# ISAB attention followed by a maxout-2 layer on one core: a searched list of work is replaced, and copies of m1 move to GpSimd

## The chip, the cores and the metric

The kernel runs on one core of a Trainium2 chip. Its time is the device time of one execution in microseconds (us); before the change the median of three runs is 314.69 us (314.38 to 314.78). One execution was recorded by the hardware profiler; all rows shown are from that trace. PE is TensorE (PEld its loading of weights), DVE is VectorE, ACT is ScalarE, POOL is GpSimd, SP the engine that issues most DMAs.

## What is computed

x has 4 batches of 12544 tokens of 128 channels; inducing has 32 rows. Two attention blocks follow each other (the 32 rows attend to x, then x attends to the 32 results), and each token then goes through a maxout of two linear maps into 1024 and a linear map back to 128.

```python
def mab(q, kv):
    s = scale * (q @ kv.transpose(0, 2, 1))
    a = np.exp(s - s.max(-1, keepdims=True))
    a /= a.sum(-1, keepdims=True) + 1e-09
    return a @ kv
h = mab(I, x)                 # [4, 32, 128]
y = mab(x, h)                 # [4, 12544, 128]
g = np.maximum(y @ w1, y @ w2)  # 1024 wide
out = g @ w_out
```

The kernel uses max(a, b) = a + relu(b - a): with w21 = w2 - w1, out = relu(y w21) w_out + y (w1 w_out). As y is a weighted mean of h, hwd = h w21 and m1 = h w1 w_out are made once for each batch (both have 32 rows, kept four times over, one copy for each quarter of the partitions), and a token needs only its 32 weights e2 (unnormalised), e2 times hwd, relu, and w_out. The division by the sum of the weights comes last, in the eviction.

## The kernel before

**Units of work.** A batch has 98 chunks of 128 tokens. Blocks take up to 16 chunks, four for each of four quarters (32 partitions each); there are 28 blocks. `stage` (word s) computes a block's 32 weights for four quarters (matmuls at L712, exponential on ScalarE). `phase` (word p) takes one piece of work from each of up to four quarters: 512 columns of e2 times hwd in a quarter of the array's rows (matmuls at L1205, all four quarters side by side), each into its own bank of PSUM, then a relu to SBUF by `relu_out`, on ScalarE (L1110) or VectorE (L1107). A piece of a phase can also be replaced by the linear part of an open group (e2 times m1, `linear_of`). `final_one` (a plain number n in the list: n of them) multiplies 128 tokens' relu by one of eight 128x128 blocks of w_out (L989); 8 of them for each chunk add up in a group's bank. There are 108 groups, each the chunks of one block and one quarter. `evict_group` multiplies a finished group by the reciprocals `rp` and writes it into one of 6 buffers of osbs, on VectorE (L1024) or, where EVICT has a 1 for that group, chunk by chunk on ScalarE (L1031); SP then stores it. The last block's groups take their linear part from m1bd by `linear_full` (L963): m1 laid out with a quarter's rows at a time and zeros elsewhere.

**First attention.** For the batches 1 to 3 it is woven into the work of the batch before. x is loaded by DMAs from GpSimd's queue (`load_x`), transposed by DMAs from SP's queue (word x), scored (c: L399, exponential on ScalarE), the exponentials are transposed by DMA (t), and multiplied with x (a: L458). Words r, e, h, w and m (`pool_rest`, `small_rep`, `small_h`, `small_hwd`, `small_m1`) finish a batch's h, hwd and m1. Word g (`turn_e2`) transposes a block's e2 by a DMA from SP's queue, and GpSimd then adds up the 32 weights of each token (L776, four halvings and den) and takes the reciprocal (L780, rd). Where that has not been done when it is needed, `dens` does it on TensorE.

**What sets the order.** All engines' instructions are in program order. The body's order is ORDER, a list of words written out by a search. The class Clock keeps a rough account of time on each engine while the program is built; it has no instructions of its own, but banks of PSUM (`bank`: the one that comes free first), the quarter that issues next and the filling with dummy matmuls (`keep_busy`) are chosen by it. PAIR is its price of a final matmul, SWITCH those of going from one layout of the array to another: full (128 rows: finals and most small matmuls), row (32 rows: phases), col (32 columns: s, c, a).

**The words in detail.** pN.V.H is a phase of N pieces; bit k of V gives the k-th piece's relu to VectorE, otherwise to ScalarE. Bit k of H holds the k-th piece: it takes two neighbouring banks, and if the next phase of the same run brings the following piece of the same quarter into the second bank, one relu takes both (128x1024, `relu_out` with two units). Any word other than p releases the held pieces as single relus (`flush`). `pick` chooses, among the quarters' next pieces, those that the finals need first. The head of the program (transposes, scores and sums of batch 0) is not in the list; the list begins about 22.7 us into the span. There H computes the second half of hwd of batch 0, V transposes w1, W multiplies it with w_out (L662).

Of the kernel before, what the change touches and what calls it, by code (L numbers as in the profile page):

```python
# [12 lines left out]
ALU = mybir.AluOpType  # L13
# [7 lines left out]
class Clock:  # L21


    PAIR = 0.0563
    COLS = 0.0566
    SWITCH = {
        "full": {"row": 0.095, "col": 0.095},
        "row": {"full": 0.082, "col": 0.088},
        "col": {"full": 0.1, "row": 0.094},
    }  # L30
    STEP = 0.0035
# [126 lines left out]
def kernel(  # L158
# [34 lines left out]
    ck = Clock()  # L193
# [73 lines left out]
    m1bd = consts.tile([128, 4, C], F16, name="m1bd")  # L267
# [3 lines left out]
    with tc.manual_schedule(engines={ET.PE, ET.DVE, ET.Activation, ET.Pool, ET.SP}):  # L271
# [25 lines left out]
        st = [dict() for _ in range(B)]  # L297
# [298 lines left out]
        def small_m1(b):  # L596
            bi, ps = bank([128, 512])
            ck.wait(max(ck.bank[bi], st[b]["hT4r"]), "p1")
            nc.tensor.matmul(out=ps[:, 0:128], lhsT=st[b]["hT4"], rhs=w1out, start=True, stop=True)
            end = ck.run(0.06)  # L600
            m1 = smp.tile([128, C], F16, name=f"m1_{b}", tag="m1")
            bd = {B - 1: [0, 1, 2, 3]}.get(b, [])
            outs = [(m1bd[32 * q : 32 * (q + 1), q, :], slice(32 * q, 32 * (q + 1))) for q in bd]
            for o, r in outs + [(m1, slice(0, 128))]:
                if b == 0:
                    nc.vector.tensor_scalar(
                        out=o, in0=ps[r, 0:128], scalar1=st[0]["rw"][r, :], scalar2=None, op0=ALU.mult
                    )
                else:
                    nc.vector.tensor_copy(out=o, in_=ps[r, 0:128])  # L610
                ck.bank[bi] = ck.on_dve(end, 0.28)
            st[b]["m1"] = m1
            st[b]["m1r"] = ck.bank[bi]

        w_of = {}
# [6 lines left out]
        def difference(eng, lo, hi, ready, us):  # L622
            eng.tensor_sub(w21[:, lo:hi], w2f[:, lo:hi], w1f[:, lo:hi])
            w_of["w21", lo] = ck.on_dve(ready, us) if eng is nc.vector else ck.on_pool(ready, us)

        def cast_w1(h):
            sl = slice(512 * h, 512 * (h + 1))
            if h == 0:
                nc.vector.tensor_copy(out=w1h[:, sl], in_=w1f[:, sl])
                ck.on_dve(20.4, 0.33)  # L630
            else:
                nc.gpsimd.tensor_copy(out=w1h[:, sl], in_=w1f[:, sl])
                w_of["cast"] = ck.on_pool(0.0, 0.8)

        def weights_2():
            turned = []
# [201 lines left out]
        bi, ps = bank([128, 512])  # L838
# [46 lines left out]
        difference(nc.gpsimd, 256, 512, 21.0, 0.64)  # L885
        load_x(1, 1)
        load_x(1, 2)
        difference(nc.gpsimd, 512, J, 22.9, 1.25)
        cast_w1(1)
        for i in range(3, 7):  # L890
            load_x(1, i)
# [82 lines left out]
        def final_one(narrow=False):  # L974
# [152 lines left out]
        def phase(n, vector=0, hold=0):  # L1127
# [195 lines left out]
```

## Time and profile before

| | |
|---|---|
| median of 3 runs | 314.69 us (314.38 to 314.78) |
| the profiled execution | 314.68 us, span 312.9 us |
| granted TensorE clock, mean | 0.998 |
| DMA | 55.69 MB, mean 178 GB/s |
| HBM | read 27.28 MB, written 25.69 MB |

The span is from the first to the last instruction; the 1.8 us between it and the execution's time lie before and after it. "Busy" is the union of the instructions' times on an engine. A group's row in the profile gives, after the shapes and the count, the busy time in us and the mean of one in ns, then the engine's idle time just before these instructions and what ended most of it. Matmuls overlap (one of 128 columns is recorded as 219 ns, and the next starts 56 ns later), so TensorE's steps are read here from starts, not from durations. A timeline row gives start, duration, engine, line, operation, output and inputs, shapes and the number of instructions merged; an idle time in front of it stands in brackets. A row of windows gives busy times of PE, PEld, DVE, ACT and POOL with counts, then the granted clock, the DMA share and GB/s. A row of DMA issues ends in the median us from issue to landing.

### The profile page before, as it was taken

Reading aid. Unit: us, or ns where it says so; the run is one execution under the profiler, and the core shown is the slowest. Engines: PE = TensorE matmul, PEld = TensorE weight load, DVE = VectorE, ACT = ScalarE, POOL = GpSimd, SP = SyncE. Lnnn points to the kernel's source line nnn. Section 1 sums busy time; section 2 is a strip of 40 time slices with the busy share of each in tenths; the row PEclk is TensorE's granted clock in tenths of the full one; section 3 lists DMA queues with packets and bytes.
Section 4 is the critical chain, followed back from the end, with each engine's and each line's share of the span. In section 5 each row is a group of like instructions: output and inputs, shape, how many; then the busy total and the mean of one; then the engine's idle time right before and its main releaser. Section 6 shows DMA issues by size and latency. Waiting matters only on the chain.

```text
span 312.9 us, 12567 instructions
## 1 busy us (share of the span) xinstructions
PE 306.0 (98%) x5316; PEld 239.4 (77%) x5316; DVE 273.1 (87%) x485; ACT 280.7 (90%) x581; POOL 122.6 (39%) x183
## 2 busy tenths in 40 slices
PE   6999999999999999999999999999999999999996
PEld 2875777777877777778877887778778877788885
DVE  2458999999889999988999998999999899989894
ACT  3668999999989989999999999989999899998875
POOL 7374007910530006677500565139205743288000
PEclk9999999999999999999999999999999999999999
DMA  7999999999399999989699999993422522342223
GB/s 206 208 255 203 218 214 192 167 231 232 107 204 244 256 212 202 212 199 218 136 241 256 185 241 200 194 229 114 131 86 103 153 102 87 118 130 103 103 88 136
DMA packets 80793, 55.69 MB, mean 178 GB/s; under 512 B 62272, under 2 KB 65632, under 8 KB 80736
## 3 DMA queue, kind: packets, MB, share of 16 engines
q1 hardware_dynamic: 74768, 41.19, 56.5%
q0 software_dynamic: 5968, 13.70, 22.6%
q8 instruction: 41, 0.67, 0.9%
q14 instruction: 16, 0.13, 0.1%
HBM read 27.28 MB, written 25.69 MB: 169 GB/s over the span
## 4 chain that ended last, share of the span: by engine, by line
PE 94%; DMA 3%; DVE 1%; issue 1%; POOL 0%; ACT 0%; POOLq 0%
PE psall L989 61%; PE psall L1205 23%; DMA xn<-in_x_dram 3%; PE psall L712 2%; PE psall L458 1%; PE psall L399 1%; PE psall L309 1%; PE psall L371 1%; PE psall L325 1%; DVE relus L1107 1%; PE psall L571 1%; PE psall L504 0%; PE psall L362 0%; DVE hwd L575 0%; PE psall L819 0%
## 5 line engine op out<-in xcount | busy, mean ns | idle before, releaser
L1110 ACT ACTIVATE relus<-psall 128x512 f16<-128x512 f32 x468 | 239.2, 620 | 15.4 <-PE psall L1205 14.4
L1107 DVE TENSOR_SCALAR relus<-psall 128x512 f16<-128x512 f32 x308 | 195.5, 683 | 16.6 <-PE psall L1205 15.7
L989 PE MATMUL psall<-woutp,relus 128*128 128x128 f16 x3104 | 203.7, 220 | 0.0
L989 PEld LDWEIGHTS <-relus 128*128 128x128 f16 x3104 | 174.9, 98 | 33.1 <-issue 27.3
L1205 PE MATMUL psall<-e,hwd 32*128 32x512 f16 (+2 forms) x840 | 81.1, 362 | 0.0
L776 POOL TENSOR_TENSOR half<-ed 128x256 f32<-128x256 f16 (+2 forms) x22 | 13.4, 611 | 145.5 <-DMA ed<-e 145.5
L780 POOL TENSOR_TENSOR rd<-den,minus 128x16 f32<-128x16 f32 (+2 forms) x22 | 57.8, 2628 | 1.7
L1024 DVE TENSOR_TENSOR osbs<-psall,rd 128x512 f32<-128x512 f32 (+1 forms) x80 | 50.9, 637 | 4.3 <-PE psall L1205 1.3
L1205 PEld LDWEIGHTS <-hwd 32*128 32x128 f16 x880 | 27.9, 91 | 11.7 <-issue 2.3
L1205 PE MATMUL psall<-m,e 32*128 32x128 f16 x372 | 36.6, 216 | 0.0
L1205 PEld LDWEIGHTS <-e 32*128 32x128 f16 x372 | 22.2, 92 | 9.6 <-issue 2.0
L776 POOL TENSOR_TENSOR half<-half 128x32 f32<-128x32 f32 (+4 forms) x66 | 21.4, 324 | 5.2
L228 POOL DMA_DIRECT2D xn<-in_x_dram x32 | 17.8, 569 | 5.7 <-DMA xn<-in_x_dram 4.3
L1024 DVE TENSOR_TENSOR osbs<-psall,rp 128x512 f32<-128x512 f32 (+3 forms) x24 | 15.6, 649 | 0.5 <-PE psall L1205 0.4
L313 DVE COPY xT<-psall 128x512 f16<-128x512 f16 (+3 forms) x12 | 5.7, 485 | 8.6 <-PE psall L309 8.4
L413 ACT ACTIVATE eu<-psall 128x512 f16<-128x512 f32 x18 | 10.8, 612 | 0.3 <-PE psall L399 0.2
L725 ACT ACTIVATE e<-psall 128x512 f16<-128x512 f32 (+2 forms) x21 | 10.9, 574 | 0.1
L316 ACT COPY xT<-psall 128x768 f16<-128x768 f16 (+3 forms) x10 | 5.8, 576 | 4.6 <-PE psall L309 4.5
L309 PE MATMUL psall<-identity,xn 128*128 128x128 f16 x98 | 7.5, 219 | 1.5 <-DMA xn<-in_x_dram 1.0
L712 PE MATMUL psall<-xT,hT 128*32 128x512 f16 (+3 forms) x110 | 8.4, 362 | 0.0
L309 PEld LDWEIGHTS <-xn 128*128 128x128 f16 x98 | 5.5, 97 | 3.1 <-DMA xn<-in_x_dram 1.4
L399 PE MATMUL psall<-xT,inducingT 128*32 128x512 f16 x72 | 6.4, 381 | 0.0
(114 smaller groups left out, 129.8 us busy)
## 6 DMA issues: line engine op xcount, KB each, us to landing
out_dram<-osbs SPq DMA_DIRECT2D x90, 256.0 KB, 2.9
xn<-in_x_dram POOLq DMA_DIRECT2D x24, 448.0 KB, 9.9
out_dram<-osbs SPq DMA_DIRECT2D x10, 128.0 KB, 4.3
relus<-in_moe_w_dram POOLq DMA_DIRECT2D x4, 256.0 KB, 5.7
xn<-in_x_dram POOLq DMA_DIRECT2D x4, 224.0 KB, 10.3
xT<-xn SPq DMA_TRANSPOSE x33, 4.3
relus<-in_x_dram SPq DMA_DIRECT2D x1, 512.0 KB, 4.0
relus<-in_x_dram SPq DMA_DIRECT2D x1, 384.0 KB, 4.4
```

What stands on the lines that cost most here:

```text
L228: nc.gpsimd.dma_start(out=xn_at[b, i][:, 0:n, :], in_=xr[b, :, k0 : k0 + n, :])
L309: nc.tensor.transpose(ps[:, j, :], xn[:, g + j, :], identity16)
L413: nc.scalar.activation(out=eu, in_=ps, func=AF.Exp, scale=scale, accum_out=st[b]["es"][:, u : u + 1])
L712: nc.tensor.matmul(out=ps[32 * q : 32 * (q + 1), 128 * t : 128 * (t + n)], lhsT=hq, rhs=xT[:, c : c + n, :], start=True, stop=True, tile_p ...
L725: nc.scalar.activation(out=blk.e2[:, 0 : 128 * wd], in_=ps[:, 0 : 128 * wd], func=AF.Exp, scale=st[0]["rs"] if blk.b == 0 else scale,)
L776: nc.gpsimd.tensor_tensor(out=dst, in0=cur[:, :, 0:n], in1=cur[:, :, n : 2 * n], op=ALU.add)
L780: nc.gpsimd.tensor_tensor(out=rp[:, 0:wd, :].rearrange("p t q -> p (t q)"), in0=den[:, 0 : 4 * wd], in1=minus1[:, 0 : 4 * wd], op=ALU.pow,)
L989: nc.tensor.matmul(out=g.ps[lo:hi, 128 * c : 128 * (c + 1)], lhsT=relu[:, lo:hi], rhs=woutp[:, jb, :], start=not g.started, stop=(state["m ...
L1024: nc.vector.tensor_mul(osb[:, 0:m, :], g.ps[:, 0 : m * C].rearrange("p (s c) -> p s c", s=m), g.blk.rp[:, t0 : t0 + m, q : q + 1].broadcas ...
L1107: nc.vector.tensor_scalar(out=dst, in0=src, scalar1=0.0, scalar2=None, op0=ALU.max)
L1110: nc.scalar.activation(out=dst, in_=src, func=AF.Relu)
L1205: nc.tensor.matmul(**seq.pop(0))
```

## The change

- Clock's prices: PAIR from 0.0563 to 0.0559, row to full from 0.082 to 0.0985, the cast of w1 on GpSimd from 0.8 to 0.62, one difference from 1.25 to 1.28, with GpSimd's clock set to 22.98 before it.
- `small_m1`: VectorE copies m1 from PSUM at once, and for the last batch the four quarters of m1bd are copied from m1 by GpSimd, instead of from PSUM by VectorE ahead of m1.
- ORDER is another list (words in the same notation). It has the same words s, c, t, a, r, e, h, w, m, H, V, W, x and g, in other places, other phases, other runs of finals, and 69 hold bits, where the list before has none.
- EVICT gives the groups 102 and 105 to ScalarE, instead of 102, 104, 105 and 107.

```diff
--- before.py
+++ after.py
@@ -21,11 +21,11 @@
 class Clock:
 
 
-    PAIR = 0.0563
+    PAIR = 0.0559
     COLS = 0.0566
     SWITCH = {
         "full": {"row": 0.095, "col": 0.095},
-        "row": {"full": 0.082, "col": 0.088},
+        "row": {"full": 0.0985, "col": 0.088},
         "col": {"full": 0.1, "row": 0.094},
     }
     STEP = 0.0035
@@ -600,15 +600,17 @@
             end = ck.run(0.06)
             m1 = smp.tile([128, C], F16, name=f"m1_{b}", tag="m1")
             bd = {B - 1: [0, 1, 2, 3]}.get(b, [])
-            outs = [(m1bd[32 * q : 32 * (q + 1), q, :], slice(32 * q, 32 * (q + 1))) for q in bd]
-            for o, r in outs + [(m1, slice(0, 128))]:
-                if b == 0:
-                    nc.vector.tensor_scalar(
-                        out=o, in0=ps[r, 0:128], scalar1=st[0]["rw"][r, :], scalar2=None, op0=ALU.mult
-                    )
-                else:
-                    nc.vector.tensor_copy(out=o, in_=ps[r, 0:128])
-                ck.bank[bi] = ck.on_dve(end, 0.28)
+            if b == 0:
+                nc.vector.tensor_scalar(
+                    out=m1, in0=ps[:, 0:128], scalar1=st[0]["rw"], scalar2=None, op0=ALU.mult
+                )
+            else:
+                nc.vector.tensor_copy(out=m1, in_=ps[:, 0:128])
+            ck.bank[bi] = ck.on_dve(end, 0.28)
+            for q in bd:
+                r = slice(32 * q, 32 * (q + 1))
+                nc.gpsimd.tensor_copy(out=m1bd[r, q, :], in_=m1[r, :])
+                ck.on_pool(ck.bank[bi], 0.3)
             st[b]["m1"] = m1
             st[b]["m1r"] = ck.bank[bi]
 
@@ -630,7 +632,7 @@
                 ck.on_dve(20.4, 0.33)
             else:
                 nc.gpsimd.tensor_copy(out=w1h[:, sl], in_=w1f[:, sl])
-                w_of["cast"] = ck.on_pool(0.0, 0.8)
+                w_of["cast"] = ck.on_pool(0.0, 0.62)
 
         def weights_2():
             turned = []
@@ -885,7 +887,8 @@
         difference(nc.gpsimd, 256, 512, 21.0, 0.64)
         load_x(1, 1)
         load_x(1, 2)
-        difference(nc.gpsimd, 512, J, 22.9, 1.25)
+        ck.pool = 22.98
+        difference(nc.gpsimd, 512, J, 22.9, 1.28)
         cast_w1(1)
         for i in range(3, 7):
             load_x(1, i)
@@ -1227,33 +1230,34 @@
 
         state["stage"] = 1
         ORDER = """
-        s p4.9 s p2.2 H1 V W p2.2 p4.2 14 m0 p3.1 4 p3.2 4 p3.3 15 p4.2 6 x1.0 2 p3.6 15 p4.8 13 p4.5 14
-        p3.1 x1.1 10 p1 p4.6 14 p4.1 20 p4.5 p2.2 16 s x1.2 s p3.5 15 p4.1 g3 18 g4 p3.4 p2.1 x1.3 11
-        x1.4 p4.5 14 p4.1 14 p3.3 10 p4.5 s c1.0 18 p2.1 g5 p3.1 x1.5 x1.6 6 x1.7 6 p4.9 11 x1.8 12 p3.6
-        p3.4 17 s c1.1 p3.4 12 x1.9 3 p4.12 3 x1.10 4 p3.2 11 p4.1 21 p4.2 p2.1 21 p4.6 t1.1 12 p1 p4.5
-        14 c1.2 c1.3 p4.10 23 p3.2 t1.3 p3.2 23 p4.3 18 p2.1 p4.8 28 p4.12 p2 23 g6 p4.5 a1.1 c1.4 a1.3
-        c1.5 p3.4 11 r1 t1.5 14 p4.8 p3.2 31 p2.1 p4.4 9 a1.5 p4.8 5 e1 17 h1 5 p4.3 p3.1 21 w1 6 s s
-        p4.10 25 p3.1 p3.4 33 p4.3 p3.1 24 s s p3.4 18 p2.2 p4.2 11 m1 13 p3.4 4 p4.12 21 p1 p3.2 15 p2.2
-        p4.2 18 p4.5 15 p1.1 p4.2 x2.0 x2.1 14 x2.2 3 p4.5 6 x2.3 13 x2.4 p4.4 p2.1 14 g9 9 x2.5 p3.6 p2
-        13 p4.9 21 p2.2 p4.2 31 x2.6 x2.7 p3.5 p4.1 26 x2.8 g10 c2.0 s p4.12 21 p2.1 p4.8 23 p4.3 10 p3.3
-        c2.1 s c2.2 13 p3.1 7 t2.1 1 p4.3 8 x2.9 2 g11 x2.10 g12 4 p4.3 16 p4.8 13 p4.12 15 p3.2 15 c2.3
-        p3.4 p3.1 28 p3.4 p3.4 22 p4.5 13 s t2.3 c2.4 a2.1 c2.5 p3.1 p3.1 21 g13 7 p2.1 t2.5 p4.2 28 p2.1
-        p4.10 6 r2 22 p3.6 p3 24 p4.1 a2.3 a2.5 p3.2 5 p4.6 14 p4.1 e2 24 p4.3 p3 12 h2 19 p4.1 p2.1 18
-        p4.10 10 p3.4 12 w2 6 p4.14 s s s 23 p2.2 p4.1 24 p3.6 s p3.2 14 p4.8 8 m2 6 p4.4 23 p3.1 p2.2 12
-        g17 2 x3.0 g15 p4.8 21 p2.1 x3.1 x3.2 p4.8 29 p3.1 x3.3 p4.10 24 p3.4 11 p4.9 x3.4 13 p4.4 16
-        p4.10 21 p3.1 p3.2 11 x3.5 x3.6 g1 g16 10 p4.1 x3.7 21 p2.1 p4.1 31 p3.2 p4.3 29 p4.5 10 x3.8
-        p3.5 s s c3.0 c3.1 13 p4.12 18 p3.3 p2 2 t3.1 9 x3.9 x3.10 3 p4.1 18 p3.5 p3 27 p4.9 p2.1 19 s
-        c3.2 c3.3 a3.1 p4.10 p2.1 19 g19 t3.3 g18 p4.9 21 p3.1 p3.1 20 p4.5 r3 21 p3.2 p3.2 31 p4.14 p3
-        27 p4.12 a3.3 c3.4 c3.5 11 p3.3 p3 8 t3.5 23 g20 p4.8 p3.3 31 p2.1 p4.8 23 p4.6 a3.5 p1 p3.4 10
-        p4.1 2 g7 1 e3 10 g14 7 h3 6 p4.3 p3.2 14 w3 3 m3 5 s s s 11 g21 p1 p4.4 21 p4.10 12 p1 p4.6 15
-        p4.8 19 p2.3 p4.2 28 g23 p2.2 p4.2 19 p3.4 3 g22 19 p3.2 p4.6 39 p3.1 p3.2 31 p4.10 p3.2 31 p4.3
-        p2 22 p4.5 11 p3.1 8 p4.1 17 p4.10 14 p3.6 s s s 11 p4.2 8 p3.5 14 g24 p4.1 16 p4.9 12 p4.1 p1.1
-        g8 23 p4.14 p2 15 s p4.1 21 p4.8 p2.1 30 g27 p4.2 p3.5 20 g26 p4.1 18 g25 3 p2.2 p4.1 31 p3.3
-        p4.4 28 p4.12 p1 17 p4.3 18 p2.2 p4.8 31 p3.4 p4.6 1 g2 30 p2.2 p4.8 31 p3.1 p4.5 32 p4.5 p2 30
-        p4.10 p2 24 p4.8 p2.1 32 p3.6 p3.1 23 p2.3 p4.1 36 p2.1 p3.1 24 p4.1 p4.7 56
+        s p3.6.4 p3.5.3 s H1 V W p2.2 p4.2 10 m0 5 x1.0 p1 p3.3 8 p3 x1.1 p2.3 17 p4.12 7 p3.2 15 p4.8 13
+        p4.12 14 p3.4 9 x1.2 p4.6 p1 14 p4.2 x1.3 21 p4.2 p2.3 18 p3.3 s x1.4 s 15 p4.2 17 p4.5 11 x1.5
+        g3 p3.3 p2.0.1 13 g4 p4.8 14 p3.5 10 p4.6 x1.6 x1.7 s c1.0 18 p2.0.1 p3.5 13 p4.10 21 p3.4 x1.8
+        p3.6.1 17 s c1.1 p3.2 x1.9 14 p4.3 10 p3.1.2 9 g5 p4.4 21 p4.1 p2.1 21 p4.5 11 p1 t1.1 p4.5 14
+        c1.2 c1.3 x1.10 p4.3 21 t1.3 p4.4 p2.1 28 p2.3.3 p4.8 25 p4.3 18 p2.1 p4.2.4 25 p4.11 c1.4 c1.5
+        a1.1 a1.3 p3 9 g6 t1.5 17 p4 p3.7 15 r1 19 p4.5.9 p2.0.3 11 a1.5 p4.1 3 e1 19 h1 3 p3.5 p4.2 10
+        w1 15 s s p4.5 24 p3.0.2 p3.2 31 p4.4.4 p3.6 12 m1 14 s s p3.1 16 p2.2 p4.2 22 p4.9 11 p3.2 13
+        p1.0.1 p3.1 15 p2.2 p4.2 19 x2.0 2 x2.1 p4.5 2 x2.2 13 p2.1.1 x2.3 p3.4 18 p4.5 10 g9 8 p4.2 p2.1
+        23 p2.1 p3.2.1 11 x2.4 p4.6 21 p2.0.2 x2.5 p4.6 32 p4.7 x2.6 p3 28 p4.5 s c2.0 1 x2.7 17 p4.3 g10
+        p2 6 x2.8 16 p4.10 10 p3.5 x2.9 c2.1 c2.2 s 16 t2.1 1 g11 p3.1 6 p4.6 14 p4.6 x2.10 15 p4.2 13
+        p4.9 g12 14 p3.1 15 s c2.3 p3.6 p3.4.4 29 p2.1 p4.4 24 p4.6 10 c2.4 t2.3 a2.1 c2.5 g13 p3.1 p3.1
+        19 t2.5 9 p4.10 p2 28 p2.2 p4.3 r2 28 p3.2 p3.2 23 p4.4 a2.3 a2.5 6 p3.1 p4.12 21 p4.2 14 e2 10
+        p3.5.1 p4.8 21 h2 9 p4.12 p2 21 p4.9 6 w2 4 p3.2 12 p4.12 s s s 22 p2.2.1 p4.2 24 p3.3 s p3.1 17
+        p4.1 15 p4.1 10 m2 10 x3.0 p3.3 x3.1 p2 10 p4.2 23 p2.2.3 g15 p4.8 x3.2 30 x3.3 p4.3 p3.2.2 28
+        p4.10 7 g16 x3.4 x3.5 p3.1 14 p4.4 8 x3.6 7 p4.12 21 p3.3 x3.7 p3 20 p4.6 9 x3.8 x3.9 12 p2.2
+        p4.8 31 p3.1 p4.9 29 p4.9 10 p3.5 c3.0 s c3.1 s 18 p4.10 12 p3.1.1 p2.1 g17 t3.1 16 p4.4 x3.10 9
+        g18 9 p3.1 p3.2 27 p4.6.4 p2.1.1 19 s c3.2 c3.3 a3.1 p4.5.1 p2.1 14 t3.3 g1 5 p4.3 8 r3 12 p3.6.7
+        p3.4 g19 20 p4.6 21 p3.2.4 p3.1 31 p3.5 p4.4 28 p4.12 c3.4 a3.3 c3.5 11 p3.3.7 p3.2.1 6 t3.5 25
+        p4.7 p3 31 p2.1 p4.4 23 p4.2 a3.5 p1.1 p3.2 14 e3 p4.2 8 h3 19 p3.3 p4.10.1 12 w3 g20 4 s s s 13
+        p2.0.2 g21 p3.4 11 m3 10 p4.9 9 g23 1 g22 1 p1 p4.10 15 p4.2 19 p2.2.1 p4.6 28 p4.12 p2 18 p3.1
+        24 p4.12.14 p3.2.4 37 p3.6.2 p3.4.2 30 p4.1 p3.1.2 31 p4.4 p2.2 21 p4.12.2 10 p3.1 12 p4.4 16
+        p4.6 10 p3.1 11 p4.5 s s 13 p3.5 10 p4.2 18 p3.6.4 g24 p2 12 p4.3 21 p2.2 p4.9 19 s s p4.4 21
+        p4.6.5 p2.2 30 p4.1 p3.5 19 g8 1 p4.5 21 p2.1.3 g14 p4.4 27 g25 5 p4.1.4 p3.2 29 p4.9.2 11 g26 p1
+        p4.9 24 g27 p2.2 p4.1 31 p4.5 p3.4.5 31 p4.0.15 p2.2 30 p4.1 p3.2 31 p4.2.1 p2.2 28 p4.12.2
+        p2.0.3 24 p2.1 p4.2 28 p2.1 p4.8 23 p2 p4.5.8 25 p4.12.8 p1 3 g2 30 p4.10 g7 p3.0.1 64
         """
 
-        EVICT = "000000000000000000000000000000000000000000000000000000000000000000000000000000000000000000000000000000101101"
+        EVICT = "000000000000000000000000000000000000000000000000000000000000000000000000000000000000000000000000000000100100"
 
         WORK = {
             "c": pool_scores,
```

## Prediction

> **What bounds the kernel now.** I read the page first (engine shares, chain of waits, costliest groups), then the waits of TensorE alone, then its timeline, to see what a step of the list costs.
>
> ```profile
> span 312.9 us, 12567 instructions
> PE 306.0 (98%) x5316; PEld 239.4 (77%) x5316; DVE 273.1 (87%) x485; ACT 280.7 (90%) x581; POOL 122.6 (39%) x183
> ...
> PE 94%; DMA 3%; DVE 1%; issue 1%; POOL 0%; ACT 0%; POOLq 0%
> ...
> L1110 ACT ACTIVATE relus<-psall 128x512 f16<-128x512 f32 x468 | 239.2, 620 | 15.4 <-PE psall L1205 14.4
> L1107 DVE TENSOR_SCALAR relus<-psall 128x512 f16<-128x512 f32 x308 | 195.5, 683 | 16.6 <-PE psall L1205 15.7
> ```
> ```profile
> PE psall L840 <- DVE ones_q L292: 1.2, 1, 1.2
> PE psall L309 <- DMA xn<-in_x_dram: 1.0, 2, 0.8
> PE psall L662 <- DVE relus L646: 0.5, 1, 0.5
> ...
> ```
>
> TensorE is 94% of the chain, and the second fence is the top of its list of waits (releaser, total, times, longest): every wait in it belongs to the head, before the final matmuls begin, and those left out are no longer than the third. ScalarE and VectorE are nearly as full, but what they wait for is TensorE's row matmuls (14.4 and 15.7 us). So the end is set by how many steps TensorE takes, not by who feeds it. What a step costs is in its timeline:
>
> ```profile
> 280.97 0.39 PE L1205 MATMUL psall<-e,hwd 32*128 32x512 f16 x4
> 281.30 1.18 PE L989 MATMUL psall<-woutp,relus 128*128 128x128 f16 x18
> 282.41 0.23 PE L1205 MATMUL psall<-m,e 32*128 32x128 f16 x1
> ...
> 282.95 1.90 PE L989 MATMUL psall<-woutp,relus 128*128 128x128 f16 x31
> 284.78 0.22 PE L1205 MATMUL psall<-m,e 32*128 32x128 f16 x1
> ```
>
> Read the starts. A row run of one round (four quarters side by side) takes 281.30 - 280.97 = 0.33 us; one of two rounds 282.95 - 282.41 = 0.54. So a further round costs 0.21, and being a run at all 0.33 - 0.21 = 0.11. The 18 final matmuls take 1.11 and the 31 take 1.83: (1.83 - 1.11)/13 = 0.055 each, and about 0.1 for turning from full to row. I use 0.327, 0.541, 0.113 and 0.095 (means over many runs). Some runs take longer than their rounds:
>
> ```profile
> 23.06 0.51 PE L1205 MATMUL psall<-e_first,hwd 32*128 32x256 f16 x9
> 23.50 0.40 PE L712 MATMUL psall<-xT,hT 128*32 128x512 f16 x4
> ...
> 188.58 0.22 PE L1205 MATMUL psall<-m,e 32*128 32x128 f16 x1
> ...
> 189.25 0.96 PE L989 MATMUL psall<-woutp,relus 128*128 128x128 f16 x14
> ...
> 305.41 0.62 PE L1205 MATMUL psall<-e,hwd 32*128 32x128 f16 x20
> ...
> 305.97 0.62 PE L989 MATMUL psall<-woutp,relus 128*128 128x128 f16 x8
> ```
>
> The first run (23.06 to 23.50) takes 0.44 instead of 0.33, that at 188.58 takes 0.67 instead of 0.54. I summed all 164 runs between the first and the last (305.41 to 305.97) from their starts: 71.7 us, where their rounds at the two prices make 70.2. These **1.5 us of short waits** are all that a better order could win without fewer steps.
>
> **The change part by part.**
>
> *The list, counted.* A run is a row of p words with only x, g and t between them; I gave each phase's jobs to quarters by the rule of pick, to see how many rounds a run has. Final matmuls (3136), stages (27), scores (18) and accumulations (9) are the same in both.
> - Row runs: 164 before (86 of one round, 77 of two, one of 1.5), 161 after (79, 81, one). At the prices: 86 x 0.327 + 77 x 0.541 + 0.434 = 70.21 against 79 x 0.327 + 81 x 0.541 + 0.434 = 70.09: **-0.12 us**. Three runs go, but one round more is needed.
> - Turns from full to row or column: 160 before, 159 after: **-0.10 us**. Column runs: 24 and 24.
>
> *Constants.* PAIR, SWITCH, the cast at 0.62, ck.pool: they steer only choices of bank and quarter while the program is written out. 0 us.
>
> *Hold bits.* None before, 69 after, but a held piece becomes one instruction over two banks only if its follower is in the next phase of the same run; by the count 17 do (12 on ScalarE, 5 on VectorE). The trace has no 128x1024 relu.
>
> ```profile
> L316 ACT COPY xT<-psall 128x768 f16<-128x768 f16 x4 | 3.2, 799 | 2.6 <-PE psall L309 2.6
> L1024 DVE TENSOR_TENSOR osbs<-psall,rd 128x256 f32<-128x256 f32 x8 | 3.3, 417 | 1.6 <-ACT osbs L1031 1.1 <-ACT relus L1110 0.6
> ```
> ```profile
> 27.57 12.88 ACT L1110 ACTIVATE relus<-psall 128x512 f16<-128x512 f32 x25
> ```
>
> ScalarE: 512 columns take 620 ns (L1110 above) and 768 take 799, so 1024 about 0.98 us; two relus back to back take 2 x 12.88/25 = 1.03, apart 1.24. So a pair saves 0.05 to 0.26 us of ScalarE; I take 0.05, the back-to-back row being the nearest, for its relus mostly follow each other. VectorE: 683 - 417 = 266 ns for 256 columns makes 1.2 us against 1.26 for two of 0.63 (the head rows below). By the Trainium skill (ScalarE: Activation LUTs, What ACT_TABLE_LOAD costs) an ACTIVATE costs 186 ns plus 0.833 ns per element and back-to-back ones overlap by 93 ns. By it a pair would save 0.09 us, 1.1 over the 12; the trace agrees for 512 columns (613 by the rule, 620 in the row), and the sum stays as it is, ScalarE not being waited for. On TensorE all this is **0**; the bounds are the 1.5 us of waits (gain) and the holds' own waits (rival 2).
>
> *Eviction.* EVICT moves the four-chunk and the one-chunk group at the very end from ScalarE to VectorE.
>
> ```profile
> 309.05 0.27 PE L963 MATMUL psall<-m1bd,e 128*128 128x128 f16 x2
> ...
> 309.42 0.42 DVE L1024 TENSOR_TENSOR osbs<-psall,rd 128x256 f32<-128x256 f32 x1 [1.05 <-ACT osbs L1031]
> ...
> 309.61 0.22 PE L963 MATMUL psall<-m1bd,e 128*128 128x128 f16 x1
> 309.86 0.37 ACT L1031 ACTIVATE osbs<-psall,rd 128x128 f32<-128x128 f32 x1 [0.62 <-PE psall L963]
> ```
> ```profile
> L1024 DVE TENSOR_TENSOR osbs<-psall,rd 128x128 f32<-128x128 f32 x4 | 1.2, 288 | 0.4 <-issue 0.2 <-PE psall L1205 0.2
> ```
>
> ScalarE begins 0.03 us after the last matmul (309.83) and takes 0.37; VectorE began 0.10 after its matmul and takes 0.29 for one chunk: 0.40 against 0.39. **0**, between -0.1 and +0.1.
>
> *m1 of the last batch.*
>
> ```profile
> 231.85 0.23 PE L1205 MATMUL psall<-m,e 32*128 32x128 f16 x1
> ...
> 232.45 1.35 PE L989 MATMUL psall<-woutp,relus 128*128 128x128 f16 x21
> ```
> ```profile
> 231.42 1.18 DVE L610 CAST m1bd<-psall 32x128 f16<-32x128 f32 x4
> ```
>
> VectorE loses the four copies, 1.18 us, behind which its next relu stood. The run at 231.85 took 0.60 for two rounds, 0.06 over; I credit that: **-0.06 us** (0 to -0.1). The four GpSimd copies are new. Bounds: 0.22 (its 128x16 addition) to 0.60 (its 128x512 cast), so 0.9 to 2.4 us together; I take 0.3 each, a quarter-partition copy being nearer to the short one.
>
> ```profile
> L632 POOL CAST relus<-relus 128x512 f16<-128x512 f32 x1 | 0.6, 604 | 0.0
> ...
> 234.47 0.67 POOL L776 TENSOR_TENSOR half<-ed 128x256 f32<-128x256 f16 x1 [9.97 <-DMA ed<-e]
> ...
> 236.47 0.22 POOL L776 TENSOR_TENSOR den<-half 128x16 f32<-128x16 f32 x1
> 236.76 2.91 POOL L780 TENSOR_TENSOR rd<-den,minus 128x16 f32<-128x16 f32 x1
> ...
> 243.74 0.67 POOL L776 TENSOR_TENSOR half<-ed 128x256 f32<-128x256 f16 x1 [4.07 <-DMA ed<-e]
> ```
>
> They wait for m1 behind g20's and g21's chains and ahead of g23's and g22's, in a queue that stood idle for 4.07 us there; m1bd is read only from 306. Without that cover g23 and g22 would come 2.4 us later; by the list g22 is issued 24 us ahead of its first eviction and needs 5.2 us for g23's chain and 8.3 of its own. **0.** Against it stands the Trainium skill (SBUF — State Buffer, SBUF: two separate sides): VectorE and GpSimd share a port pair, which one instruction holds to its end while the other is blocked. Read at its widest it would hold VectorE back up to 2.4 us here, 1.2 more than the copies it loses; this trace shows no such hold-up:
>
> ```profile
> L1107 DVE TENSOR_SCALAR relus<-psall 128x512 f16<-128x512 f32 x7 | 4.4, 685 | 0.3 <-PE psall L1205 0.3
> ...
> 176.00:181.00 5.00, 5.00 (x83) 3.99 (x79) 4.97 (x9) 4.90 (x10) 4.68 (x6) 1.00 0.96 162
> ```
>
> In these 5 us GpSimd worked for 4.68, and VectorE's relu took 685 ns against 683 in the whole run.
>
> *Order around the head.*
>
> ```profile
> 23.63 1.89 DVE relus L1107 x3
> ```
>
> On the chain of waits VectorE's three first relus (0.63 each) come here, and behind them on its queue H1's copy and V's copy, for which L662 waits (the 0.5 above). The new list again gives VectorE three pieces ahead of H1 (two of six go to ScalarE as a pair, one alone). **0**, between -0.1 and +0.63 (one relu more in front).
>
> *Transposes and divisions.* They are moved on SP's queue. With TensorE's words priced as above, the shortest lead of an x before the first scores that need it is 7.3 us (x2.6 to c2.2; before 8.0), of a g before its first eviction 12.3 (g20; before 15.4).
>
> ```profile
> xT<-xn SPq DMA_TRANSPOSE x33, 4.3
> ed<-e SPq DMA_TRANSPOSE x22, 3.1
> ```
>
> From issue to landing they take 4.3 and 3.1 us, and a division needs 5.2 of GpSimd more (234.47 to 239.67), 8.3 together. Some leads are longer than before, some shorter; all still cover. **0.**
>
> Sum: -0.12 - 0.10 - 0.06 = -0.28 us, from the profiled execution's own 314.68 (its span of 312.9 and 1.8 around it): **314.4 us**. The median of the runs shown, 314.69, is the same.
>
> **Rivals.** About 0.2%, 0.63 us, is what a measurement of this kernel can tell from no change.
> 1. *The short waits go too.* The new constants are nearer to the trace (0.0559 against 0.055 to 0.056 measured), so banks may be chosen better. All 1.5 us: 314.4 - 1.5 = 312.9; two thirds: 313.4. For it: waits of 0.1 us are spread over some twenty runs. Against it: pieces lie as far ahead of their first use in both lists (median 7.8 and 7.7 us), so no more slack was made.
> 2. *Held banks make TensorE wait* (slower). A hold takes the two neighbouring banks that come free first, not the freest bank, and keeps one until the second is full; place: the run after each of the 17 pairs. Price by the row at 188.58: 0.13 each, 17 x 0.13 = 2.2: **316.6**. It decides from (0.63 + 0.28)/17 = 0.054 us a pair; if all 69 bits cost 0.13, it is 323. For it: eight banks, two of them with open groups. Against it: no wait of that size after most runs now.
> 3. *Divisions come late* (slower): g25, g26 and g27 stand within 5.5 us of TensorE's time, and GpSimd needs 5.2 for each. g26 would be done 8.3 + 5.2 = 13.5 us after g25 is issued and is wanted 18.0 after it. From a slip of 4.5 us on, VectorE waits in its eviction, and the relus behind it; a slip of 6.5 gives 314.4 + 2 = 316.4. For it: SP's queue is in order, and a store ahead of g25 that waits for its eviction holds it up. Against it: in this trace GpSimd waits for these transposes, VectorE never for GpSimd.
>
> **How the numbers follow.** No change that can be told 0.40 (314.4, own range 313.9 to 315.2), rival 1 0.32 (about 313.3), rival 2 0.20, rival 3 and the head's 0.63 0.08. So faster 0.32, same 0.40, slower 0.28. The range leaves out the lower tenth (rival 1 in full) and most of rival 2 beyond its price: 313.0 to 316.4.
>
> **What would show it.** Right: about 161 row runs of 0.33 or 0.54 us, TensorE's waits still only in the head, 12 and 5 relus of 128x1024, four casts of m1bd on GpSimd in idle time, five chunk evictions on ScalarE instead of ten. Wrong: row runs whose sum lies more than 2.5 us over 70.1 (rival 2) or less than 0.5 (rival 1), VectorE waiting for GpSimd's rd (rival 3), or matmuls of L989 farther apart than 0.056 us.

## The result and the profile after

| | before | changed |
|---|---|---|
| median of 16 runs each, same chip | 314.64 us (314.23 to 315.25) | 316.34 us (314.87 to 318.62) |
| ratio, 95% interval | | 1.0051 (1.0031 to 1.0070) |
| the profiled execution | 314.68 us, span 312.9 | 314.87 us, span 313.1 |

The change is slower by half a per cent, and its runs lie over 3.75 us where those of before lie over 1.0. The profiled execution is the quickest of the 16, so its trace shows the least of what costs time. Its page, the parts that answer to those quoted of before:

```profile
span 313.1 us, 12566 instructions
PE 307.7 (98%) x5317; PEld 240.2 (77%) x5317; DVE 270.5 (86%) x475; ACT 280.6 (90%) x566; POOL 124.0 (40%) x187
...
PE 89%; DMA 7%; POOL 2%; issue 1%; DVE 0%; SPq 0%; POOLq 0%; DVEq 0%
```

ScalarE and VectorE issue 25 instructions fewer; the DMA share of the chain of waits went from 3% to 7% (2.1 points of it are loads of the weights in the head, 1.6 the tile xT). The groups of instructions (line, engine, operation, count, busy us, mean ns, idle before):

```profile
L1113 ACT ACTIVATE relus<-psall 128x1024 f16<-128x1024 f32 x13 | 13.4, 1031 | 0.0
L1110 DVE TENSOR_SCALAR relus<-psall 128x1024 f16<-128x1024 f32 x5 | 6.1, 1218 | 0.8 <-PE psall L1208 0.6
...
L612 POOL COPY m1bd<-m 32x128 f16<-32x128 f16 x4 | 1.2, 288 | 0.2
```

18 held pairs became one relu of 128x1024, and the four GpSimd copies take 0.29 us each. As in the prediction, I cut TensorE's time into runs by start (a run's time is the next run's start less its own) and summed them by kind. Finals are counted to the next matmul's start, so that their turns are in them; columns have the head's in them:

```
us, all runs of a kind      before  changed  after_base  sp_fix3  no_holds  later_use
row runs (phases)            71.72    71.63       71.64    71.62     74.19      75.07
final matmuls               191.83   191.99      192.42   191.76    192.40     191.67
column runs (s, c, a)        16.01    16.31       16.65    16.12     17.89      16.01
```

(The four on the right are experiments.) The row runs are 161 and did what was counted: 70.09 by their rounds and 1.54 of short waits, where before had 70.21 and 1.51. What grew are runs of finals and columns, and only a few of them. One experiment below, sp_fix3, has the same list on every engine but SP, so its final matmuls can be set against those of the changed kernel one by one, from the starts in both traces. In this execution the changed kernel falls behind it at two places: 0.27 us at c2.2 (124.3), the first reader of x2.6, and 0.24 at r3 (206.3), the first reader of x3.10; elsewhere behind the first final the distance moves by less than 0.1. after_base, a run of the same work that took 315.57, falls behind by 0.30 at c2.2, by 0.31 at a3.1 (203.3), the reader of t3.1, and by 0.68 at r3.

At c2.2 the transpose x2.6 is this row of SP's timeline:

```profile
120.21 1.36 SPq L241 DMA_TRANSPOSE xT<-xn  x1
```

It landed at 124.59, and c2.2's last two matmuls started at 124.63, 0.29 us behind its first two; in sp_fix3 its four start together.

At r3 the changed kernel's chain of waits is (start, us, what):

```profile
200.28 0.70 DVE osbs L1027
200.99 0.12 SPq L1052
...
201.19 5.05 DMA xT<-xn
206.24 0.05 issue
206.29 0.21 PE psall L424 x2
```

Read it upwards. L424 is word r3, the scores of batch 3's last two chunks. It starts 0.05 us after the last transposed tile, x3.10, has landed. That transpose was issued at 201.19 because SP, just ahead of it, had to issue a store, and that store waited for its eviction on VectorE. SP's issues there, first of the changed kernel, then of before:

```profile
193.06 2.12 SPq L241 DMA_TRANSPOSE xT<-xn  x1
195.29 2.49 SPq L1052 DMA_DIRECT2D out_dram<-osbs  x3
197.90 1.24 SPq L769 DMA_TRANSPOSE ed<-e  x1
199.22 1.25 SPq L439 DMA_TRANSPOSE eT<-eu  x1
200.57 0.53 SPq L1052 DMA_DIRECT2D out_dram<-osbs  x1
201.19 1.72 SPq L241 DMA_TRANSPOSE xT<-xn  x1
```
```profile
195.03 0.92 SPq L1049 DMA_DIRECT2D out_dram<-osbs  x1
196.06 1.70 SPq L439 DMA_TRANSPOSE eT<-eu  x1
197.87 4.19 SPq L241 DMA_TRANSPOSE xT<-xn  x2
```

Before, t3.1 (L439) and then x3.9 and x3.10 follow each other, done by 202.06, with no g between them. In the new list SP issues here without a pause, and the 33 transposes of x take between 1.2 and 3.1 us of it each (least, median and most, in ns, of the changed kernel's tile xT; before, 1247, 1328 and 3492):

```profile
L241 SPq DMA_TRANSPOSE xT<-xn x33: 1247/1568/3119, 26.5 to 201.2; - x33
```

Three stores, g17, t3.1 and one more store stand between x3.9 and x3.10. From a tile's landing to its first reader's start there were, worked out from both traces, 3.13 us for x3.10 and 2.22 for t3.1 before, and 0.05 and 0.22 in the changed kernel: in this execution they land just when they are wanted, and any delay is TensorE's.

### The profile page after: what moved, and what is told of

It reads as the page before. It is cut to its first block, busy times and chain, and to the rows that moved or that the text cites. A ratio compares the mean times of both kernels' runs of the same rounds, so it can differ in the third digit from the quotient of the medians.

```text
span 313.1 us, 12566 instructions
## 1 busy us (share of the span) xinstructions
PE 307.7 (98%) x5317; PEld 240.2 (77%) x5317; DVE 270.5 (86%) x475; ACT 280.6 (90%) x566; POOL 124.0 (40%) x187
## 4 chain that ended last, share of the span: by engine, by line
PE 89%; DMA 7%; POOL 2%; issue 1%; DVE 0%; SPq 0%; POOLq 0%; DVEq 0%
PE psall L992 60%; PE psall L1208 22%; DMA xn<-in_x_dram 3%; DMA relus<-in_moe_w_dram 2%; PE psall L714 2%; DMA xT<-xn 2%; PE psall L399 1%; PE psall L458 1%; POOL xn L228 1%; POOL w L625 1%; PE psall L571 1%; PE psall L621 0%; DVE osbs L1027 0%; PE psall L504 0%; PE psall L821 0%
## 5 line engine op out<-in xcount | busy, mean ns | idle before, releaser
L1113 ACT ACTIVATE relus<-psall 128x512 f16<-128x512 f32 (+1 forms) x456 | 239.1, 632 | 16.7 <-PE psall L1208 15.5
L1110 DVE TENSOR_SCALAR relus<-psall 128x512 f16<-128x512 f32 (+1 forms) x302 | 195.0, 692 | 20.2 <-PE psall L1208 18.1
L1027 DVE TENSOR_TENSOR osbs<-psall,rd 128x512 f32<-128x512 f32 (+1 forms) x82 | 51.8, 632 | 4.8 <-PE psall L966 1.6
L309 PE MATMUL psall<-identity,xn 128*128 128x128 f16 x98 | 8.2, 230 | 0.4 <-DMA xn<-in_x_dram 0.3
L309 PEld LDWEIGHTS <-xn 128*128 128x128 f16 x98 | 6.2, 104 | 2.3 <-DVE xn L838 0.8
```

What stands on the lines that cost most here:

```text
L309: nc.tensor.transpose(ps[:, j, :], xn[:, g + j, :], identity16)
L1027: nc.vector.tensor_mul(osb[:, 0:m, :], g.ps[:, 0 : m * C].rearrange("p (s c) -> p s c", s=m), g.blk.rp[:, t0 : t0 + m, q : q + 1].broadcas ...
L1110: nc.vector.tensor_scalar(out=dst, in0=src, scalar1=0.0, scalar2=None, op0=ALU.max)
L1113: nc.scalar.activation(out=dst, in_=src, func=AF.Relu)
```

## Experiments

Each was run beside the kernel before on one chip; the ratio is to that. A word x, t or g stands for one DMA transpose on SP. From sp_none on, the function that a word x or t calls is split: for chosen tiles the DMA itself is issued by a word y or u, while x or t does only the account of Clock. So the words' order on every engine but SP stays the same; the lines move by 8 to 13 (L407 is c, L432 r, L471 a, L1065 the store).

**Which part of the change?** First the change once more, and then the list and EVICT of before with the new constants and the copies on GpSimd:

```diff
-        ORDER, EVICT of the change
+        ORDER, EVICT of before
```

> The changed kernel as it is, for a second profiled execution. Theory T (TensorE waits for transposes on SP's queue that land about when they are wanted: x2.6 for c2.2, x3.10 for r3): the time again lies between 314.9 and 318.6 us, and in a slower execution than the first profiled one (314.87) the added time stands in front of c2.2, r3 or another reader of a transposed tile. Rival H (held pieces keep banks): the added time stands in row runs longer than 0.54 us, spread over the body.

> The list and EVICT of before, with the change's constants and its copies of m1. Theories T and H: 314.4 to 314.8 us, narrow, the list being the cause. Rival M: about 316.3 us.

after_again: 315.59 us (315.02 to 316.55), 1.0023 (1.0007 to 1.0039). old_list: 314.81 us, 0.9998 (0.9984 to 1.0012). So the new list, with its EVICT, costs the time; copies and constants cost nothing that can be told. What the list costs differs between series of runs: 1.0023 here, 1.0051 in the result, 1.0058 and 1.0052 below for the same work of the engines. In after_again TensorE's waits hold a line that the trace of before does not have:

```profile
PE psall L424 <- DMA xT<-xn: 0.3, 1, 0.3
```

**Holds or tiles?** no_holds takes all 69 hold bits out. later_use gives two late tiles time by moving their readers:

```diff
-p3.2.4
+p3.2
...
-c2.1 c2.2 s 16
+c2.1 s 16
...
-8 r3 12 p3.6.7 p3.4 g19 20
+20 p3.6.7 p3.4 g19 20 r3
```

> The changed kernel with all 69 hold bits taken away, otherwise the same list. Theory T: about 316.3 us as before, spread as wide. Rival H: 314.5 us and narrow.

> c2.2 is moved 8 us later (to c2.3) and r3 3 us later; the x words stay. Theory T: 314.4 to 315.0 us with a spread under 1 us. Rival H: still about 316.3 us with a spread of 3 to 4. Rival M (the GpSimd copies of m1 and the constants): still about 316.3.

no_holds: 318.42 us, 1.0114 (1.0087 to 1.0141), which neither theory had said. later_use: 318.4 us, 1.0107 (1.0082 to 1.0132), against what my theory said. The groups of row matmuls of the changed kernel, of no_holds and of later_use:

```profile
L1208 PE MATMUL psall<-e,hwd 32*128 32x512 f16 (+2 forms) x840 | 80.9, 361 | 0.0
```
```profile
L1208 PE MATMUL psall<-e,hwd 32*128 32x512 f16 (+2 forms) x840 | 83.1, 361 | 0.5 <-DVE relus L1110 0.2
```
```profile
L1208 PE MATMUL psall<-e,hwd 32*128 32x512 f16 (+2 forms) x840 | 82.8, 361 | 1.3 <-DVE relus L1110 0.8 <-ACT relus L1113 0.5
```

Without holds these matmuls are busy 2.2 us longer, and the sums by kind above say how the span came from 313.1 to 318.3: +2.56 in row runs, +1.58 in column runs, +0.41 in finals, +0.63 in the rest. The profiled execution of no_holds is the slowest of its six (320.04 us), that of the change its quickest, and the column runs' part is mostly tiles again (1.0 us of waits for xT at c, by TensorE's list of waits). The row runs' part is the holds': they save TensorE time. In later_use the tiles' wait is gone (column runs -0.30, finals -0.32), but row runs gained 3.44: to move a word is to move everything around it. Relus that held banks account for 1.3 us of that by the row above; where the rest comes from isn't shown. That is why the next experiments move SP's DMAs alone.

**SP's order alone.** sp_none is the split without a moved tile; sp_early moves seven tiles ahead (x3.10 right behind x3.9, t3.1 ahead of g17, five of batch 2); sp_early_b3 only the two of batch 3. sp_late puts two tiles of the list *before* later. The edit of sp_early_b3, then that of sp_late:

```diff
-x3.8 x3.9 12
+x3.8 x3.9 y3.10 12
...
-g17 t3.1
+u3.1 g17 t3.1
```
```diff
-x2.6 x2.7 p3.5
+x2.6 x2.7 y2.6 p3.5
...
-g19 t3.3
+y3.10 g19 t3.3
```

> The changed kernel, with the issue of a transpose and its entry in the program's own account of time in two functions; every engine's program is that of the change. 315.2 to 316.6 us, spread 1.5 to 4: what the next two are compared with on the same chip.

> Only SP's order differs: x2.4, x2.5, x2.6, x2.10, x3.10, t3.1 and t2.5 are issued earlier by one to eight us; the work of TensorE, ScalarE and VectorE and its banks stay. Theory T: 314.4 to 314.9 us, spread under 1 us, no wait of TensorE on a transposed tile. Rival E (engines and banks of the new list, not the transposes, vary): 315.2 to 316.6, as wide as without.

> Only x3.10 and t3.1 earlier. Theory T: between the two, some 0.3 to 0.8 us below the change alone, as the waits before c2.2 stay. Rival E: no difference.

> The kernel before, with x2.6 issued after x2.7 and x3.10 issued after the three stores behind it (about 4 us later); nothing else moved. Theory T: 315.2 to 316.5 us, TensorE waiting at r3 and c2.2, and a wider spread than before. Rival E: 314.7 us as before.

sp_none: 316.25 us, 1.0058 (1.0039 to 1.0076), with L432 waiting 0.7 us for xT. sp_early, meant as the cure: 321.19, 1.0199 (1.0181 to 1.0218); sp_early_b3: 320.32, 1.0178 (1.016 to 1.0195). sp_late: 314.85, 1.0003 (0.9994 to 1.0012): its two tiles still landed 0.01 us too late and 0.87 us early, a dose that decides nothing. TensorE's longest wait in sp_early and in sp_early_b3:

```profile
PE psall L471 <- DMA eT<-eu: 4.0, 1, 4.0
```
```profile
PE psall L471 <- DMA eT<-eu: 3.4, 1, 3.4
```

L471 is a3.1, reader of t3.1. x3.10, now ahead, pushed t3.1, which is wanted first, back to an issue at 202 us. Both runs are slower than sp_none, where theory T had said faster. The cure of one tile was the next one's wait: the theory's place was right, my remedy wrong.

**Which tile first?** sp_fix issues t3.1 behind x3.9 and x3.10 ahead of g17, with the five of batch 2; sp_fix_b3 only those two. In the list before, t31_late puts t3.1 behind x3.9, and t31_later behind x3.10. The edits of sp_fix_b3 and of t31_later:

```diff
-c3.1 s 18 p4.10 12 p3.1.1 p2.1 g17
+c3.1 s u3.1 18 p4.10 12 p3.1.1 p2.1 y3.10 g17
```
```diff
-t3.1 9 x3.9 x3.10 3
+t3.1 9 x3.9 x3.10 u3.1 3
```

> The changed kernel with only SP's order altered: t3.1 directly behind x3.9 (ahead of three stores and g17), x3.10 behind those stores and ahead of g17, and x2.4, x2.5, x2.6, x2.10 and t2.5 earlier as in sp_early. Theory T2 (SP's queue is in order and full; what stands last in it reaches TensorE just in time or late, and a wait of 3 us halves the clock for a while): every transposed tile lands 1.5 us or more ahead of its reader, 314.3 to 314.9 us, spread under 1. Rival E (banks and engines of the new list vary): 315.2 to 316.6.

> Only t3.1 and x3.10 moved, as in sp_fix. Theory T2: the waits before a3.1 and r3 go, those before c2.2 stay (0.3 to 1 us): 314.6 to 315.4. Rival E: 315.2 to 316.6.

> The kernel before with t3.1 issued behind x3.9 instead of ahead of it, some 3 us later; nothing else moved. Theory T2: it lands 0.3 to 1 us after a3.1 could begin: 315.0 to 316.0 us and a spread of 1.5 or more. Rival E: 314.7 as before.

> The kernel before with t3.1 issued behind x3.9 and x3.10, some 5 to 6 us later. Theory T2: a wait of about 3 us before a3.1, and a granted clock of about 0.5 for 3 to 7 us behind it (1.7 to 3.4 us more): 318 to 321 us. Rival E: 314.7 as before.

sp_fix: 315.25, 1.0018 (1.0005 to 1.0032); sp_fix_b3: 315.9, 1.0037 (1.0017 to 1.0057): medians below sp_none's, but above what theory T2 had said, and not cured. In sp_fix nothing is lost at c2.2 any more, but x3.10, still behind x3.9, is issued at 200.10 and lands at 206.41, too late for r3:

```profile
PE psall L432 <- DMA xT<-xn: 0.6, 1, 0.6
```

t31_late: 315.01, 1.0011 (0.9997 to 1.0024), the tile 0.04 us ahead of its reader. t31_later: 319.09, 1.0146 (1.0114 to 1.0179), as theory T2 had said. One DMA moved behind two others in the kernel before makes it slower by more than the change did. The longest wait of t31_later and its chain:

```profile
PE psall L471 <- DMA eT<-eu: 2.6, 1, 2.6
```
```profile
201.53 3.76 DMA eT<-eu
205.29 0.04 issue
205.34 0.63 PE psall L471 x32
```

**The cure.** after_base is sp_none's work again. sp_fix2 and sp_fix3 set the order by each tile's due time; sp_fix3's words, with sp_fix4 as sp_fix3 but x2.6 one store later:

```diff
-p1 t1.1
+p1 y1.10 t1.1
...
-g9 8 p4.2 p2.1 p3.2.1 11 x2.4
+y2.4 g9 8 p4.2 p2.1 p3.2.1 11 y2.5 y2.6 x2.4
...
-t2.1 1 g11
+t2.1 1 y2.10 g11
...
-c2.5 g13
+c2.5 u2.5 g13
...
-c3.1 s 18
+c3.1 s u3.1 y3.10 18
...
-p4.4 x3.10
+p4.4 y3.9 x3.10
```

> The changed kernel (its engines' programs unchanged) on the same chip, for the comparison: 315.2 to 316.6 us, spread 1.5 to 4.

> The changed kernel with another order on SP alone: x3.10 and x3.9 change places (c3.4, the reader of x3.9, comes 9 us after r3), t3.1 ahead of g17 and a store, x2.5 and x2.6 one store earlier, x2.10 ahead of t2.1 and g11, x1.10 ahead of t1.1, t2.5 ahead of g13. Theory T2: every transposed tile lands 1 us or more ahead of its reader, 314.2 to 314.8 us with a spread under 1, which is the time of before or 0.3 less. If instead 315.0 to 315.4 as in sp_fix, some 0.5 us of the change's loss is not SP's.

> The changed kernel, SP's order alone altered again: x3.9 goes to the end, so that t3.1 and x3.10 follow x3.8 with only the stores between them that are older; x2.10 stays behind t2.1 as in sp_fix, x2.5, x2.6 and x1.10 earlier as in sp_fix2. Theory T2: what is gained in sp_fix up to the 1800th final matmul (0.3 us) and in sp_fix2 behind it (1.0 against after_base) adds up: 314.2 to 314.7 us, spread under 1.2. If the rest is not SP's: 315.0 to 315.4 again.

> As sp_fix3, with x2.6 one store later, where sp_fix has it. Theory T2: 0 to 0.3 us more than sp_fix3, by waits before c2.2.

| | median us (range), 12 runs each | ratio to before |
|---|---|---|
| after_base | 316.34 (314.99 to 317.40) | 1.0052 (1.0034 to 1.0070) |
| sp_fix2 | 315.10 (314.27 to 316.24) | 1.0009 (0.9997 to 1.0021) |
| sp_fix3 | 314.30 (314.24 to 314.69) | 0.9984 (0.9976 to 0.9993) |
| sp_fix4 | 314.83 (314.26 to 315.28) | 1.0000 (0.9991 to 1.0009) |

sp_fix2 missed: x2.10 now stood ahead of t2.1, and a2.1, the reader of t2.1, waits for it:

```profile
PE psall L471 <- DMA eT<-eu: 0.8, 1, 0.8
```

sp_fix3 puts t2.1 first again and came out as theory T2 had said; sp_fix4 loses 0.53 us to it in the median, more than the 0.3 foreseen, and its profiled execution shows no wait for a tile. With SP's order alone changed, 2.04 us go from after_base to sp_fix3, and the spread with them, 2.4 us to 0.45. (They ran on two chips; the kernel before had 314.69 us on the one and 314.67 on the other.) sp_fix3 is 0.37 us faster than before and beats both kernels. Its span is 312.6 us. SP's issues in the same stretch:

```profile
193.64 1.55 SPq L1065 DMA_DIRECT2D out_dram<-osbs  x2
195.29 2.23 SPq L447 DMA_TRANSPOSE eT<-eu  x1
197.95 1.53 SPq L243 DMA_TRANSPOSE xT<-xn  x1
199.58 1.02 SPq L1065 DMA_DIRECT2D out_dram<-osbs  x1
200.69 1.22 SPq L782 DMA_TRANSPOSE ed<-e  x1
202.01 0.53 SPq L1065 DMA_DIRECT2D out_dram<-osbs  x1
202.63 2.54 SPq L243 DMA_TRANSPOSE xT<-xn  x1
```

t3.1 goes at 195.29 (199.22 in the changed kernel), x3.10 at 197.95 (201.19), and x3.9, wanted later, last. What TensorE does at r3, first in the changed kernel, then in sp_fix3:

```profile
205.60 0.62 PE L992 MATMUL psall<-woutp,relus 128*128 128x128 f16 x8
206.29 0.21 PE L424 MATMUL psall<-inducingT,xT 128*128 128x32 f16 x2
```
```profile
205.33 0.62 PE L1005 MATMUL psall<-woutp,relus 128*128 128x128 f16 x8
205.79 0.20 PE L432 MATMUL psall<-inducingT,xT 128*128 128x32 f16 x2
```

Eight finals from start to start take 0.69 us, then 0.46: 0.23 of it was the wait, too short for the list of waits.

## Why the prediction was wrong

It said 314.4 us and no change that can be told; it is 316.34. That this lies close to the prices of rivals 2 and 3 (316.6 and 316.4) is luck: neither held banks nor late divisions made the loss. Its steps in order:

- *What bounds the kernel*: held. TensorE is 98% busy, and with the tiles in time (sp_fix3) the waits in its list lie in the head alone.
- *The list, counted* (-0.12 and -0.10): its size held. sp_fix3 against before has row runs -0.10 and finals, with their turns, -0.07 us in the sums by kind, but column runs +0.11.
- *The sum of -0.28*: sp_fix3's median is 0.37 below before, but that the sizes are alike is in part luck. In the two profiled executions the time from the first row run to the last matmul is the same, 286.5 us. The first row run itself starts 0.25 us earlier in sp_fix3 (22.81 against 23.06), which is not the list's: with one and the same head it starts anywhere from 22.8 to 23.2 in these traces. And the quickest executions are 0.20 apart (314.24 against 314.44); the rest of the 0.37 is that the times of before spread more.
- *Rival 1, short waits go*: wrong, 1.54 us against 1.51.
- *Hold bits* (0; 0.98 and 1.2 us each; 17 pairs): 1031 ns, 1218 ns and 18 pairs. *Rival 2, holds cost 2.2 us*, has the wrong sign: with the holds taken out, row runs take 2.56 us more. I compared this list with the one before, where I should have asked what this list is without them.
- *Eviction and constants* (0): old_list at 0.9998 bounds the constants; EVICT was replaced with the list and wasn't tried by itself, but from the last matmul's start to the end of the span there are 3.3 us in both kernels (before 312.9 - 309.61, now 313.1 - 309.84).
- *m1* (0.3 us each, hidden): held, 0.288 each (the row of L612 above), at 242.59 to 243.92, with the first reader of m1bd at 306.66. The credit of 0.06 us was too small to be measured by itself.
- *Head* (0, between -0.1 and +0.63): the chain went another way, over the second half of w2 - w1 on GpSimd, and the first final starts 0.33 us earlier than before (27.77). 0.14 of that is the list's order, 4.56 us from the first row run to the first final against 4.70; the rest lies ahead of the list. The changed kernel's chain, then its timeline:

```profile
22.96 1.30 POOL w L625
```
```profile
27.44 0.38 PE L992 MATMUL psall<-woutp,relus 128*128 128x128 f16 x4
```

- ***Transposes and divisions* ("all still cover. 0.") is the step that failed.** It put this term at 0, and after_base to sp_fix3 measures it at 2.04 us. The lead of a tile was counted in TensorE's time, from its word to its first reader's, and set against 4.3 us from issue to landing. That a word's DMA is issued when its word comes was taken for granted. But SP issues in order, a transpose of x takes it 1.2 to 3.1 us, and it holds at a store whose eviction isn't done. Of the 7.3 us that the prediction gave x2.6, the shortest, about 3.2 were gone when SP came to it (TensorE is at its word at 117.0, SP at 120.21) and 4.4 more until it landed: c2.2 waited 0.29. x3.10's word comes 8.8 us ahead of r3 (197.48 in TensorE's timeline); behind six others it was issued 3.7 us later (201.19) and took 5.05 to land, so nothing was left. Before, SP was as late with it (4.0 us), but the word came 12.2 ahead, and 3.1 were left. Nor did the prediction give a lead to any t word, and t3.1 had 0.22 us left. Rival 3 named the mechanism, SP in order and a store ahead, but put it on the divisions, and I gave it 0.08 with the head. Its place was wrong: in the changed kernel no engine's list of waits has one for GpSimd's divisions.
- *What would show it*, "TensorE's waits still only in the head": in the profiled execution that was nearly so, and it misled; after_again, sp_none and after_base show the line for xT, after_base with this:

```profile
PE psall L432 <- DMA xT<-xn: 0.5, 1, 0.5
...
```
```profile
201.27 0.53 SPq L1065
...
201.89 5.04 DMA xT<-xn
206.94 0.05 issue
206.99 0.21 PE psall L432 x2
```

SP came to x3.10 0.70 us later than in the changed kernel's profiled execution (201.89 against 201.19), and r3 0.70 later.

Shown: the list costs the time (old_list), and SP's order of issue is all of it (after_base to sp_fix3). Not shown: what makes an execution take 317 or 318 us, since none such of the changed kernel was profiled. The one at 318.62 us has a mean granted clock of 0.995, as t31_later's profiled one has, and all others 0.998 to 1.000; so a wait long enough to lower the clock, as told below, fits that one execution, but not those at 317. Why landing times differ between executions is open too. The DMA engines are full there (the DMA share in windows, which can go above 1, is 1.27 for 200 to 205 us in the changed kernel, 1.20 before and 1.13 in sp_fix3), which fits, but no run took that load away. How the 2.04 us of the medians divide between batch 2's tiles and batch 3's wasn't settled: sp_fix_b3 (1.0037) and sp_none (1.0058) have intervals that overlap. In the profiled executions it is 0.3 us for batch 2 (c2.2), and for batch 3 0.24 us in the quickest and 1.0 in after_base's.

## What to carry to other kernels

When transposes or stores move in an in-order queue, make a ledger for that queue: each DMA's issue time, the waits of the stores ahead of it, its time to landing, and then what each reader has left. With 0.05 and 0.22 us left for two tiles, the profiled execution was 0.2 us above before and the median 1.7; where the line lies wasn't found (0.87 us left in sp_late cost nothing that could be told). Order such a queue by when tiles are wanted, and move the DMA alone when you test it. A wider spread of the times can be the sign of a tile that lands when it is wanted: here it went with the loss.

## What had not been expected of the hardware

A long wait of TensorE costs more than itself. Windows of t31_later around its 2.6 us (from:to, length, then busy PE, PEld, DVE, ACT and POOL with counts, granted clock, DMA share, GB/s):

```profile
203.00:205.00 2.00, 0.00 (x0) 0.00 (x0) 0.25 (x1) 0.88 (x4) 0.00 (x0) 1.00 1.13 175
...
206.00:207.00 1.00, 1.00 (x12) 0.57 (x9) 0.91 (x3) 0.62 (x2) 0.00 (x0) 0.70 1.02 300
207.00:208.00 1.00, 1.00 (x12) 1.00 (x10) 1.00 (x3) 0.96 (x2) 0.00 (x0) 0.50 0.88 168
208.00:209.00 1.00, 1.00 (x11) 0.48 (x8) 0.24 (x1) 0.00 (x0) 0.72 (x2) 0.50 1.05 192
209.00:210.00 1.00, 1.00 (x14) 0.88 (x11) 0.79 (x2) 0.75 (x2) 0.84 (x3) 0.59 0.64 125
210.00:212.00 2.00, 2.00 (x42) 1.79 (x39) 1.24 (x3) 1.16 (x3) 1.84 (x3) 1.00 0.00 0
```

About 1 us after work began again the granted clock fell to 0.50 and stayed there 3.4 us (206.4 to 209.8). Half of 3.4 and the 2.6 make 4.3 us; the span grew by 4.0 (316.9 against 312.9). In sp_early, with a wait of 4.0 us, it fell before the wait was over and was 0.50 for 6.8 us; sp_none's wait of 0.7 us left the mean clock at 1.000. The Trainium skill (TensorE: Matmul & The Clock Gate, Part 1) has the clock at half after an idle window of about 3.4 us, and full again after as much work; the 3.4 us at half agree, but here 2.6 us without a matmul were enough.
